# Pacing the loads of a fused attention and mixture-of-experts kernel by memsets on VectorE, with a third buffer for values

## The chip, the cores and the metric

The kernel runs on one core of one Trainium2 chip. Five engines take part: TensorE (PE in the profile; PEld is its weight load), VectorE (DVE), ScalarE (ACT), GpSimd (POOL) and SyncE (SP). SP computes nothing; it issues nearly all DMA transfers, in the order of the program. The metric is the time of one execution on the device in microseconds (us), as a median over runs.

## The reference

Block-sparse attention over 4 batches, 8 heads, 768 positions and 64 channels, followed by a mixture of 8 experts in which each token goes to one expert. Positions form 24 blocks of 32. A query block sees its own block and its two neighbours, the first and the last block, and three drawn blocks; the first and the last query block see everything.

```python
mask = np.abs(blk_i - blk_j) <= 1
mask = mask | (blk_i == 0) | (blk_j == 0) | (blk_i == n_blocks - 1) | (blk_j == n_blocks - 1)
for qb in range(n_blocks):
    for kb in sampled_blocks[qb]:
        mask[qb*32:(qb+1)*32, kb*32:(kb+1)*32] = True
scores = np.where(mask, scale * q @ k.T, -1e9)
x = softmax(scores) @ v                      # heads side by side: 3072 tokens x 512
e_idx = np.argmax(x @ w_gate + modality_bias[modality_id], axis=1)
out[e_idx == e] = gate_w * (np.maximum(x @ w1[e], 0) @ w2[e])
```

## The kernel before

**Attention by tiles.** The batches are worked in two halves of two batches. In each half the two outer query blocks (0 and 23) are the dense part, 8 items of two heads; the other 22 query blocks go two at a time as 11 sparse tiles, so there are 22 sparse tiles, g = 0 to 21. A sparse tile has four items, (n, b): query block n of the pair, batch b of the half. All items stand in one list of 104: first the 8 dense items of half 0, then the 88 sparse ones, with the 8 dense items of half 1 put in two at a time after the sparse items 21, 29, 45 and 47 (DENSE_AFTER).

**Ticks.** The list is run as a software pipeline. In tick t the step `op` is made for the item t - LAG[op]: for a sparse item the scores S (L528) at its own tick, the mask M (L536, VectorE) one later, the exponential X (L544, ACT) two, the transposes T (L553) and their copy A (L558, ACT) four, the weighing W of shared values (L575) five, the weighing V of own values (L584) seven, the division O (L438) eight, a turning Y ten, and the gate G (L601) thirteen later. W, V, O, Y and G are made once per tile, at its last item. Within a tick the order is `OXTSMGVAYW`, with numbered places between; `side(t, f, place)` hangs other work on a place of a tick. The first 14 ticks are written out by hand as a list of tokens (START). The order of each engine's instructions is the order of the program (a manual schedule); semaphores come from the data alone. So SP, which has no part in the arithmetic, issues a load as soon as it has come to it and its buffer is free.

**Loads of a sparse tile**, all on SP. With `last(g)` the tick of a tile's last item:

- Queries, `fetch_q` (L142), 256 KB into one of three `q_raw` buffers, with the drawn block numbers read into registers (`own_numbers`, L508), at last(g-2), place 3. For tiles without dense items between them this is 5 ticks ahead of the tile's first scores.
- Neighbour values, `fetch_v` (L486 to L492), two loads of 128 KB, at last(g-2) + 8. In the first two tiles of a half two more loads bring the blocks 0 and 23, which then stay in the buffer; the other two neighbour blocks are copied from the buffer of the tile before by GpSimd, `share_v` (L499), at last(g-2) + 11.
- Own (drawn) values, `fetch_own` (L516), six loads of 128 KB, at last(g-2) + 9 and + 10.

The value buffers `vbuf` are two, slots 7 and 8, so the loads of tile g wait until tile g-2 has been weighed, which is at last(g-2) + 7. The weighing of the tile's own values is at last(g-2) + 15 where no dense items come between, that of the shared ones two earlier. Keys lie in the chip as a whole (`kd`); `share_k` (L462 to L477, GpSimd) copies those of a tile together.

**Dense loads of half 1**: keys (L154) and values (L160) in pieces of 256 KB, at ticks written in DENSE_IN, 14 to 59.

**Probabilities**: the copies A go to `at`, five buffers, for sparse items (L558) and to `ad`, four buffers cut from slot 4, for dense ones (L414).

**From attention to experts.** When both tiles of a pair have been gated, a generator `routing` is put in a queue (`fillers`) of which a few steps are made in each tick (ten in half 0, seven in half 1). It chooses the expert, computes the gate weight (`write`, L311), lets LATER = 19 steps pass, issues two x writes of 256 KB to `x_d` in DRAM (L323), and then goes on to rank the rows (`chain`, `rank`). When 16 of the 24 row tiles are ranked, `choose(0)` picks the expert with the most rows; with that begins `early_groups`, stepped once per tick. It fetches the first weights (`fetch`, L704 and L708, 512 KB each, two at its first step, the third to fifth at its ticks 6, 9 and 12), splits each into two parts (L712 ACT, L713 VectorE or GpSimd) and gathers the rows of group 0 (`gather`, L718). Its matmuls (L736 to L738, L751 to L753) begin when the last tile has been weighed. Then 10 further groups of 256 rows and a last half group follow, each with 8 weights of 512 KB.

**Slots** are pieces of on-chip memory of 12 KB per partition, used one after another: 0, 1, 2 and 9 for dense keys, 2 and 3 for dense values, 4 for `ad`, 5 and 6 for the sparse keys, 7 and 8 for sparse values; later all of them for weights and rows (`expert_slots`).

## Time and profile before

| | us |
|---|---|
| median of 3 runs (lowest, highest) | 546.74 (543.19, 548.45) |
| the profiled execution | 548.88 |
| its span, first to last instruction | 547.1 |
| mean granted TensorE clock | 0.986 |
| DMA on SP's queue | 105.02 MB, 64.1% of 16 engines' span |

The profiled execution is the source of all rows. Its time is 1.8 us more than its span and 2.1 us more than the median. The page gives busy time per engine and 40 slices of 13.7 us, in which a digit is a tenth. A row of the timeline is start, duration, engine, line, operation, and in brackets the idle time before it with what ended it: `[0.86 <-DMA slot<-v]` is 0.86 us in which TensorE waited for a load of values. "Issue" is idle time for which the profile shows no releaser. SPq is SP's queue of DMA issues. Attention runs until about 240 us, the first two groups of the experts until about 290, the rest to the end.

### The profile page before, as it was taken

The numbers are of one execution on the slowest core, as the hardware profiler recorded it, in microseconds if no ns is written. First come the engines' busy times: TensorE is split into PE (matmuls) and PEld (weight loads), VectorE is DVE, ScalarE is ACT, GpSimd is POOL, SyncE is SP. The second block draws the span as 40 slices with busy tenths as digits, with TensorE's granted clock in tenths as the row PEclk, the third lists the DMA queues.
The fourth block names the chain that finished last, engine by engine and source line by source line (L and its number), as shares of the span: only waits on it lengthen the run. The fifth ranks groups of instructions, "written<-read, shape, count | busy, mean of one in ns | idle before, by whom it ended". The sixth has DMA issues, their size and how long they took to land.

```text
span 547.1 us, 18936 instructions
## 1 busy us (share of the span) xinstructions
PE 517.6 (95%) x7274; PEld 435.0 (80%) x7274; DVE 373.2 (68%) x1129; ACT 337.4 (62%) x768; POOL 222.2 (41%) x453
## 2 busy tenths in 40 slices
PE   7999899999999997889999999999999999999994
PEld 5567666777778775778879898998989899898973
DVE  4895667778679997776984756556566555656652
ACT  2789866978878987644444555545455554654561
POOL 1758754867458884540454031230303203031121
PEclk9899999999999999799999999999999999999998
DMA  8994898869975779936778875766758566675730
GB/s 283 307 237 120 243 229 223 241 190 231 224 207 144 200 205 270 239 97 248 266 250 268 278 248 187 253 218 229 244 173 269 191 228 236 220 242 191 258 121 22
DMA packets 48690, 119.43 MB, mean 218 GB/s; under 512 B 7632, under 2 KB 7760, under 8 KB 48592
## 3 DMA queue, kind: packets, MB, share of 16 engines
q1 hardware_dynamic: 44512, 105.02, 64.1%
q0 software_dynamic: 4080, 13.12, 6.6%
q8 instruction: 59, 0.97, 0.8%
q14 instruction: 39, 0.32, 0.2%
HBM read 105.52 MB, written 12.86 MB: 216 GB/s over the span
## 4 chain that ended last, share of the span: by engine, by line
PE 71%; DVE 10%; DMA 8%; issue 5%; POOL 2%; ACT 1%; SPq 1%; POOLq 1%; DVEq 0%; ACTq 0%
PE bank L753 8%; PE bank L752 7%; PE bank L751 7%; PE bank L736 7%; PE bank L738 7%; PE bank L737 7%; PE bank L553 5%; PE bank L528 5%; DMA slot<-v 4%; PE bank L575 2%; PE bank L584 2%; PE bank L725 2%; DMA slot<-kD 2%; DVE slot L713 2%; PE bank L601 2%
## 5 line engine op out<-in xcount | busy, mean ns | idle before, releaser
L713 DVE TENSOR_TENSOR slot<-slot 128x1024 fp32r<-128x1024 f32 x96 | 120.2, 1257 | 92.5 <-ACT slot L712 92.3
L712 ACT CAST slot<-slot 128x1024 fp32r<-128x1024 f32 x104 | 108.1, 1048 | 103.0 <-PE bank L737 50.7
L738 PE MATMUL bank<-slot 128*128 128x256 f32 x384 | 107.8, 281 | 0.9 <-DVE slot L713 0.9
L736 PE MATMUL bank<-slot 128*128 128x256 f32 x384 | 108.4, 282 | 0.0
L737 PE MATMUL bank<-slot 128*128 128x256 f32 x384 | 107.6, 280 | 0.0
L762 POOL DMA_INDIRECT out<-slot,si x21 | 21.2, 1008 | 184.1 <-ACT slot L758 181.1
L544 ACT ACTIVATE a<-y,mn 128x256 f32<-128x256 f32 x176 | 88.6, 510 | 7.1 <-DVE mn L536 6.9
L753 PE MATMUL bank<-slot 128*128 128x512 f32 x200 | 79.1, 396 | 1.3 <-DVE slot L744 1.3
L751 PE MATMUL bank<-slot 128*128 128x512 f32 x200 | 80.0, 400 | 0.0
L752 PE MATMUL bank<-slot 128*128 128x512 f32 x200 | 79.1, 395 | 0.0
L738 PEld LDWEIGHTS bank<-slot 128*128 128x128 f32 x384 | 72.2, 188 | 1.1 <-DVE slot L713 1.1
L736 PEld LDWEIGHTS bank<-slot 128*128 128x128 f32 x384 | 72.2, 188 | 0.6
L737 PEld LDWEIGHTS bank<-slot 128*128 128x128 f32 x384 | 72.2, 188 | 0.4
L536 DVE CUSTOM_DVE_ANT_1 y<-bank,smask 128x256 f32<-128x256 f32 x176 | 66.1, 417 | 0.5
L477 POOL COPY slot<-slot 128x128 f32 x264 | 63.6, 294 | 6.0 <-issue 6.0
L558 ACT COPY at<-bank 128x512 f32<-128x512 f32 x88 | 50.7, 577 | 11.8 <-PE bank L553 11.7
L499 POOL TENSOR_SCALAR slot<-slot 32x1024 f32<-32x1024 f32 x40 | 41.7, 1042 | 29.9 <-PE bank L584 11.6
L553 PE MATMUL bank<-ident,a 128*128 128x128 f32 x352 | 53.2, 284 | 0.2 <-DVE mn L536 0.2
L528 PE MATMUL bank<-slot,q_raw 64*32 64x256 f32 x1408 | 50.3, 382 | 1.8 <-DMA q_raw<-qH 0.8
L753 PEld LDWEIGHTS bank<-slot 128*128 128x128 f32 x200 | 37.6, 188 | 10.8 <-DVE slot L744 1.7
L752 PEld LDWEIGHTS bank<-slot 128*128 128x128 f32 x200 | 37.6, 188 | 8.1 <-DVE slot L713 0.4
L751 PEld LDWEIGHTS bank<-slot 128*128 128x128 f32 x200 | 37.6, 188 | 7.9 <-ACT slot L911 0.3
(290 smaller groups left out, 849.9 us busy)
## 6 DMA issues: line engine op xcount, KB each, us to landing
slot<-w SPq DMA_DIRECT2D x105, 512.0 KB
slot<-v SPq DMA_DIRECT2D x180, 128.0 KB
x_d<-xr SPq DMA_DIRECT2D x22, 256.5 KB
q_raw<-qH SPq DMA_DIRECT2D x22, 256.0 KB
slot<-v SPq DMA_DIRECT2D x16, 256.0 KB
slot<-kD SPq DMA_DIRECT2D x13, 256.0 KB
slot<-v SPq DMA_DIRECT2D x4, 768.0 KB
slot<-kD SPq DMA_DIRECT2D x3, 768.0 KB
```

The lines of the kernel that those rows point to most:

```text
L528: nc.tensor.matmul(sp[u][32 * pr:32 * pr + 32, b * 256:(b + 1) * 256], lhsT=q[r, b * NPAIR + pr, n, :], rhs=kv[r, s0:s0 + 8, b, pr, :], st ...
L536: nc.vector.tensor_tensor_reduce(y[:, u, :].rearrange("p (s f) -> p s f", s=8), sp[u][:, b * 256:(b + 1) * 256].rearrange("p (s f) -> p s ...
L544: nc.scalar.activation(a[:, u, :], y[:, u, :], AF.Exp, bias=mn[:, u:u + 1], scale=-1.0, accum_out=total[:, u:u + 1])
L553: nc.tensor.transpose(tp[:, k:k + P], a[:, u, c * P:(c + 1) * P], ident)
L712: nc.scalar.copy(h, staged(n))
L713: (eng or (nc.gpsimd if n in POOL_SPLITS else nc.vector)).tensor_tensor(l, staged(n), h.bitcast(F32), ALU.subtract)
L736: nc.tensor.matmul(o, lhsT=h[:, fs], rhs=xh[g % 2][:, c, :], start=c == 0 and f % 2 == 0, stop=False)
L737: nc.tensor.matmul(o, lhsT=h[:, fs], rhs=xl[g % 2][:, c, :], start=False, stop=False)
L738: nc.tensor.matmul(o, lhsT=l[:, fs], rhs=xh[g % 2][:, c, :], start=False, stop=c == 3 and f % 2 == 1)
L751: nc.tensor.matmul(o, lhsT=hh[0][:, f, ts_], rhs=h[:, fs], start=f == 0, stop=False)
L752: nc.tensor.matmul(o, lhsT=hh[0][:, f, ts_], rhs=l[:, fs], start=False, stop=False)
L753: nc.tensor.matmul(o, lhsT=hl[f // 4][:, f % 4, ts_], rhs=h[:, fs], start=False, stop=f == 7)
```

## The change

- **Pacing.** `pace(spot)` is a memset of one element on VectorE. It is put ahead of query loads (from tile 2 on), of the second neighbour load (L492) and of each of the two groups of own loads (from tile 2 on), on an element that the load then overwrites. The load so waits until VectorE has come to that place in its own program.
- **Third buffer.** `vbuf` has three buffers (slots 8, 7, 4). The two neighbour loads go to last(g-2) + 4 and + 7, the own loads to + 5 and + 6. The blocks 0 and 23 are loaded in the first three tiles of a half.
- **Probabilities.** `ad` is gone; dense and sparse items share six `at` buffers.
- **x writes.** The 19 steps go, and ranking follows at once. `put_row` hangs the two writes of a pair on ticks 2 past a multiple of 4 (counted from the first sparse tick), four ticks apart; past tick NI + 8 they are issued at once. `gather` asserts that the rows it needs have been written.
- **First weights.** Until attention ends, `load` makes one fetch per step, and each is half a weight (256 KB).
- **Slots.** The tables of the beginning are in slot 9, the first two weight stages and gathered rows in slot 0 in place of 4, and the split weights in slot 4 in place of 0.

```diff
-VL = (8, 1)
+VL = ((4, 7), (7, 1))
 VS = (11, 7)
-VG = ((9, 6), (10, 3))
+VG = ((5, 1), (6, 1))
...
-NAT, NXR = 5, 5
-LATER = 19
+NAT, NXR = 6, 5
+XD = (2, 6)
...
-        vbuf = [slot(7 + n)[:, 0:3072].rearrange("p (c f) -> p c f", c=3) for n in range(2)]
+        vbuf = [slot(n)[:, 0:3072].rearrange("p (c f) -> p c f", c=3) for n in (8, 7, 4)]
...
+        def pace(spot):
+            nc.vector.memset(spot, 0.0)
+
-        def fetch_q(half, m):
+        def fetch_q(half, m, paced=False):
             q_raw = work.tile([P, 2, HB * NPAIR * 32], F32, name="q_raw", bufs=3)
+            if paced:
+                pace(q_raw[0:1, 0, 0:1])
             nc.sync.dma_start(q_raw.rearrange("p n f -> p (n f)"), qH[half, m])
...
-        blk_raw = const.tile([P, NB * 3 * 2], I32, name="blk_raw")
+        setup = slot(9)
+        blk_raw = setup[:, 0:NB * 6].bitcast(I32)
...
-            for _ in range(LATER):
-                yield
             for n in range(2):
-                nc.sync.dma_start(x_d[(tau + n) * P:(tau + n + 1) * P, :], xrs[n])
+                put_row(n, tau + n, xrs[n])
...
-        def fetch_v(m, half):
+        def fetch_v(m, half, ns=(0, 1)):
             i, g = 2 * m + 1, half * NM + m
-            vg = vbuf[g % 2]
+            vg = vbuf[g % 3]
...
-            if m < 2:
+            if m < 3 and 0 in ns:
...
-            nc.sync.dma_start(vg[0:32, 2, :], vrow[:, i + 2, :])
-            nc.sync.dma_start(vg[96:P, 1, :], vrow[:, i + 1, :])
+            for n in ns:
+                vn = vg[0:32, 2, :] if n == 0 else vg[96:P, 1, :]
+                if n and g > 1:
+                    pace(vn[0:1, 0:1])
+                nc.sync.dma_start(vn, vrow[:, i + 2 - n, :])
...
+            if g > 1:
+                pace(vg[32 * n:32 * n + 1, 2 * n, 0:1])
+            for k in ks:
+                reg = own[g][3 * n + k]
                 nc.sync.dma_start(vg[32 * (k + n):32 * (k + n) + 32, 2 * n, :], vrow[:, bass.ds(reg, 1), :].rearrange("p j f -> p (j f)"))
...
-            def load(nf, ns):
+            def load(nf, ns, slow=False):
...
-                        fetch(f)
-                        now["fetch"] += 1
+                        if slow or now["half"]:
+                            fetch(f, now["half"])
+                            now["half"] ^= 1
+                        else:
+                            fetch(f)
+                        now["fetch"] += not now["half"]
+                        if slow:
+                            return
...
-                load(p + 2, p)
+                load(p + 2, p, True)
...
+        def put_row(n, tau, xr):
+            def put():
+                nc.sync.dma_start(x_d[tau * P:(tau + 1) * P, :], xr)
+                written.add(tau)
+            t_ = t + 1
+            while (t_ - at["s", 0, 0, 0, 0]) % 4 != XD[0]:
+                t_ += 1
+            t_ += 4 * n
+            if t_ < NI + 8:
+                side(t_, put, XD[1])
+            else:
+                put()
+
         def q_load(m, half):
-            qraw[m, half] = fetch_q(half, m)
+            qraw[m, half] = fetch_q(half, m, (m, half) > (1, 0) or half > 0)
```

## The prediction

> **What bounds the kernel now.** I read the page first (busy time, slices), then the table of windows by stage, then the timelines of TensorE and of SP's queue where TensorE is idle, and last the groups of VectorE.

> ```profile
> span 547.1 us, 18936 instructions
> ...
> PE 517.6 (95%) x7274; PEld 435.0 (80%) x7274; DVE 373.2 (68%) x1129; ACT 337.4 (62%) x768; POOL 222.2 (41%) x453
> ...
> PE   7999899999999997889999999999999999999994
> ...
> PEclk9899999999999999799999999999999999999998
> DMA  8994898869975779936778875766758566675730
> ```

> TensorE is busy for 95% of the span, so at most some 30 us are there to win, and the slices say where: at the very start, in slices 5 to 7, and in slices 15 to 17, where the granted clock falls too. Where the DMA digits are 9 the PE digits drop.

> ```profile
> 60.00:110.00 50.00, 45.93 (x1108) 33.63 (x1098) 35.76 (x156) 38.03 (x123) 31.44 (x85) 1.00 0.90 238
> 163.90:193.60 29.70, 29.70 (x839) 23.34 (x837) 27.14 (x127) 26.24 (x86) 25.05 (x68) 1.00 0.60 165
> 193.60:224.40 30.80, 24.68 (x691) 19.02 (x692) 27.23 (x135) 23.95 (x75) 19.73 (x39) 1.00 0.94 248
> 224.70:231.60 6.90, 6.90 (x75) 6.40 (x67) 4.27 (x13) 3.38 (x9) 4.44 (x3) 0.51 0.93 239
> 231.60:239.70 8.10, 7.32 (x236) 6.33 (x234) 6.24 (x45) 5.49 (x13) 0.88 (x1) 1.00 0.59 152
> 239.70:292.60 52.90, 50.58 (x375) 44.74 (x374) 39.67 (x103) 22.72 (x31) 19.57 (x12) 1.00 0.66 229
> 292.60:530.00 237.40, 237.40 (x1537) 214.91 (x1537) 144.30 (x154) 125.03 (x154) 50.98 (x43) 1.00 0.68 227
> ```

> Columns: stretch, its length, busy us (and count) of PE, PEld, DVE, ACT, POOL, granted clock, DMA share, GB/s. From 292.6 on TensorE never stops: the experts are bound by it, and whatever is won before passes through to the end one for one. Stage 163.9 to 193.6 is also full. The losses: 50.00 - 45.93 = 4.07 us in 60 to 110; 30.80 - 24.68 = 6.12 us in 193.6 to 224.4; 6.90 us at a clock of 0.51, which is 0.49 x 6.90 = 3.4 us; 8.10 - 7.32 = 0.78 us after that; 52.90 - 50.58 = 2.3 us in 239.7 to 292.6. What the second and fourth consist of:

> ```profile
> 163.84 1.08 PE L584 MATMUL bank<-slot,at 128*32 128x64 f32 x64
> 193.60:224.40 30.80, 24.68 (x691) 19.02 (x692) 27.23 (x135) 23.95 (x75) 19.73 (x39) 1.00 0.94 248
> ...
> 201.14 0.25 PE L568 MATMUL bank<-rexp,fold 128*32 128x8 f32 x8 [0.39 <-ACT at L558]
> 202.40 1.09 PE L584 MATMUL bank<-slot,at 128*32 128x64 f32 x62 [0.86 <-DMA slot<-v]
> 211.10 0.36 PE L584 MATMUL bank<-slot,at 128*32 128x64 f32 x2 [0.63 <-DMA slot<-v]
> 212.85 1.09 PE L584 MATMUL bank<-slot,at 128*32 128x64 f32 x62 [1.39 <-DMA slot<-v]
> 215.73 1.10 PE L528 MATMUL bank<-slot,q_raw 64*32 64x256 f32 x32 [0.76 <-DMA q_raw<-qH]
> 218.03 0.92 PE L575 MATMUL bank<-slot,at 128*64 128x64 f32 x24 [0.35 <-issue]
> 224.40 0.42 PE L584 MATMUL bank<-slot,at 128*32 128x64 f32 x14 [1.64 <-issue]
> 238.63 1.09 PE L584 MATMUL bank<-slot,at 128*32 128x64 f32 x62 [0.79 <-issue]
> ```

> The first two rows are the weighing of own values (L584) of tiles 12 and 16: four tiles in 29.76 us, so 7.44 us for a tile and 1.86 us for a tick (four to a tile). After them the weighing of tiles 17 and 18 waits for value loads (0.86 + 0.63 + 1.39 = 2.88 us), the scores of tile 21 wait 0.76 us for queries, and 0.39 + 0.35 + 1.64 + 0.79 = 3.17 us are ACT and "issue". Why the loads are late stands in SP's queue:

> ```profile
> 181.65 0.38 SPq L491 DMA_DIRECT2D slot<-v  x1
> 189.96 0.35 SPq L491 DMA_DIRECT2D slot<-v  x1
> 198.82 0.38 SPq L491 DMA_DIRECT2D slot<-v  x1
> 202.34 0.91 SPq L704 DMA_DIRECT2D slot<-w  x2
> 203.44 3.38 SPq L516 DMA_DIRECT2D slot<-v  x6
> 209.88 0.35 SPq L142 DMA_DIRECT2D q_raw<-qH  x1
> ...
> SPq L491 <- PE bank L584: 15.4, 5, 5.6
> ```

> L491 is the first value load of a tile. With two buffers it may go only when the tile two before has been weighed: five waits, 15.4 us. From tile 16 on SP is simply slower than TensorE: L491 at 181.65 and 198.82 is 17.17 us for two tiles, 8.59 us each with one pair of x writes, against 7.44. So it falls behind 1.15 us per tile until, at 202.34, two weights of 512 KB go in ahead of tile 19's six own loads.

> **The change, part by part.** *Third buffer, earlier loads.* Own loads move from ticks 9 and 10 to 5 and 6 after the last item of the tile two before, and the weighing stands at tick 15: their lead grows from 5 or 6 ticks (9.3 us) to 9 or 10 (17 us). The neighbour loads gain 4 ticks and 1. At 203.44 the own loads took 3.38 us to issue, and the slowest row for a landing is the queries' (issued at 209.88, waited for until 215.73: 5.85 us). 17 us hold both and over 7 us of lateness besides, so I take the 2.88 us as gone (ends: 0 and 2.88).

> *SP's queue.* The change removes nothing from it: eight value loads, one query load with its register load, and one x write per tile are still issued, and four more value loads (rows 0 and 23 for a third buffer) and five more halves of weights come in. Each paced load now waits for VectorE, and all later entries stand behind it: own loads, x writes, weights and dense keys. The loads with the shortest lead are the queries, 5 ticks or 9.3 us, unchanged. From tile 15 to the query load of tile 21 SP can lose 5 x 1.15 = 5.8 us and 4 halves x 0.91/2 = 1.8 us (row at 202.34), 7.6 us; with 5.85 us of landing that is 4.1 us more than the lead. The wait for tile 21's queries, 0.76 us now, is then between 0 and 4.1 us; SP loses part of this lateness wherever the dense items lengthen a tile, so I take the middle, 2.0 us: cost 1.3 us net.

> *Memsets.* 20 for queries, 19 for neighbour values, 40 for own values: 79 on VectorE, four to a tile.

> ```profile
> L214 DVE MEMSET smask<- 128x1 f32 x1 | 0.1, 59 | 0.1
> L444 DVE RECIPROCAL rd<-rd 128x1 f32<-128x1 f32 x16 | 2.6, 164 | 0.6
> ...
> 150.88 1.07 PE L584 MATMUL bank<-slot,at 128*32 128x64 f32 x60
> 152.77 0.31 PE L584 MATMUL bank<-slot,at 128*32 128x64 f32 x4 [0.82 <-issue]
> ```

> A memset of one column took 59 ns: 79 x 59 = 4.7 us, and 4 x 59 = 0.24 us per tile. VectorE idles (29.70 - 27.14)/4 = 0.64 us per tile in the full stage, so it is hidden; at the price of the next small operation (164 ns) it would be 0.66 us and just not. Should VectorE wait in a memset, the masked scores (L536) behind it stop, then ACT, then TensorE. What it must wait for is old: the weighing three tiles back lies two ticks earlier in program order, and GpSimd's sharing of that buffer four ticks. I take 0.3 us; ends 0 and 4.7, all of it.

> *Dense and sparse probabilities share six buffers in place of five and four.* Counting allocations, only one is tight: tile 12's first copy (L558) must now wait for tile 11's weighing of the same tick. The last two rows are that weighing; until now the copy could run beside it. Between 0 and the 2.2 us from 150.88 to 153.08; ACT has two ticks until its next result is due, so 0.3 us.

> *x writes.* Issued two ticks after the gates or more, one by one, in place of 19 steps later, as a pair. Same bytes, same queue, 0; the rows are gathered later still. Because those steps no longer stand ahead of the ranking, the choice of the first expert and its weights come about 19/7 = 2.7 ticks (5 us) earlier, and that lies in the same crowded stretch; its price is in SP's 7.6 us. *Weights in halves:* one half a tick in place of 512 KB at once; the bytes between two value loads halve. *Small tables in slot 9, first stages in slot 0, weights in slot 4:* the slots are free long before; 0.

> *Issue and ACT waits* (3.17 us): no part of the change names them, but they stand where the DMA share is 0.94. Between 0 and 3.17; half, 1.6 us.

> *The dense stretch.* Of the 4.07 us in 60 to 110 the rows give one load wait:

> ```profile
> 92.23 0.66 PE L375 MATMUL bank<-slot,qd 64*64 64x256 f32 x8 [0.43 <-DMA slot<-kD]
> ```

> 0.4 us for dense keys, taken as gone. The rest waits for banks and engines. Ends: 2 us gained, or 2 us lost if the start, where SP now waits for the memsets of tiles 2 and 3 in place of running ahead, hands on its lateness.

> *Clock.* 3.4 us at 0.51. It fell at 224.7, after 6.1 us of gaps in 31 us, and was 1.00 in all full stages; I take it as back. [...]

> **The sum.** 2.9 + 1.6 + 3.4 + 0.4 - 1.3 - 0.3 - 0.3 = 6.4 us gained. The profiled execution took 548.9 us, 2.1 us over the median of the runs shown (546.74), so it gives 542.5 for itself; carried to the median, 540.3, and I say 540.5.

> **The rivals.** *Clock stays low* (0.15): all else as above, 540.3 + 3.4 = 543.7. For it: the last two tiles leave TensorE little to do with or without waits. *The waits only move* (0.13): DMA runs at 248 GB/s and a share of 0.94 in 193.6 to 224.4, and the weights now begin 5 us sooner in just that stretch. If the value waits and the clock stay, the sum is 0.1: 546.6. Against it: DMA's share is 0.60 in the 30 us before, room for loads that come earlier. *SP's queue becomes the bound* (0.13), the other side: paced by VectorE it can't use a quiet moment, and at 8.59 us a tile the query loads turn late after (9.3 - 5.85)/1.15 = 3 tiles. It decides once the query waits pass the 4.9 us won elsewhere without the clock. With tiles 14 to 21 and the halves that is 8 x 1.15 + 1.8 - 3.45 = 7.6 us, and 2 us in the dense stretch, 4 with the memsets in full: 11.6 to 13.6, less 4.9: 6.7 to 8.7 us slower, 554. Against it: own loads no longer hold SP up, 15.4 us of waits. *Everything clears* (0.15): SP's lateness is absorbed, all of 2.88 + 0.76 + 3.17 + 3.4, and 2 us of the dense stretch: 12.2 us, 534.5. The forecast keeps 0.44.

> **How the numbers follow.** About 1% (5.5 us) is what a measurement of this kernel can tell from no change: under 541.3 is faster, over 552.2 slower. Faster: 0.6 of the forecast's 0.44, the 0.15 of the full clearing and a little of the clock's: 0.43. Slower: most of SP's 0.13: 0.11. Within 1%: 0.46. The forecast's own range, by its ends, is 536 to 545. From 533.5 to 549 it takes in the clearing, the clock and the moved waits, and leaves out SP's case and tails.

> **What would show it.** L584 without a DMA wait after 193.6, tiles 7.4 us apart up to the last: the buffer is right. A wait of L528 on q_raw of 1 to 3 us at tile 20 or 21: SP's term is right; such waits from tile 15 on, or before 110 us, make SP the bound and me wrong. VectorE's memsets at some 60 ns with no idle time before them on PE or POOL: the pacing is free. The clock at 1.00 up to the first expert matmul, which comes at 239.7 now and should come near 234: the clock's term. If the first expert matmul comes earlier by what I say but the end does not, the stage up to 292.6 has taken it back.

## The result, and the profile after

The changed kernel took 570.33 us (median of 4 runs, 568.22 to 576.74), the kernel before 545.50 us on the same chip (median of 4, 543.19 to 548.45). The ratio is 1.0425, with a 95% interval of 1.0364 to 1.0486: some 23 us slower. The prediction said 540.5, and not over 549. The profiled execution took 571.51 us. Ratios leave out executions counted as slow (here the one of 576.74), which the medians include; the profiles of e3 and e14 below are of such executions.

In code and profile the lines have moved: masked scores L536 are now L543, scores L528 are L535, the weighing of own values L584 is L591, sharing of values L499 is L503 and of keys L477 is L476, queries L142 are L145, own loads L516 are L523, the gather L718 is L731, the split L712 and L713 are L724 and L725, the x write L323 is L1192. The memsets are L139. Experiments shift them by up to five more.

The page of the changed kernel, to be set against the page shown ahead:

```profile
span 569.6 us, 19125 instructions
...
PE 521.2 (92%) x7274; PEld 436.5 (77%) x7274; DVE 377.3 (66%) x1209; ACT 338.1 (59%) x768; POOL 223.8 (39%) x452
...
PE   7798798989999998588889999999999999999994
...
PEclk9999798999999999689999999999999999999998
```

TensorE's busy time grew by only 3.6 us, from 517.6 to 521.2, while the span grew by 22.5. So TensorE stands idle for longer, and where it is busy part of that is at half clock (0.50): the PEclk row has dents in slices 5, 7, 17 and 18, where before there were two, in slices 2 and 17. To find where the time goes, take the start of each tile's weighing of own values (the first row of its block at L584 or L591 in TensorE's timeline):

| tile | before, us | after, us | later by |
|---|---|---|---|
| 1 | 51.8 | 53.3 | 1.5 |
| 2 | 59.6 | 68.1 | 8.5 |
| 7 | 113.8 | 122.3 | 8.5 |
| 8 | 121.1 | 132.9 | 11.8 |
| 12 | 163.8 | 175.6 | 11.8 |
| 18 | 211.1 | 226.5 | 15.4 |
| 19 | 221.5 | 248.8 | 27.3 |
| first expert matmul | 239.7 | 260.3 | 20.6 |
| last matmul | 539.1 | 561.6 | 22.5 |

Three steps stand out: tile 2 (7 us), tile 8 (3.3 us, and 3.6 more between 12 and 18), and tile 19 (11.9 us, of which 6.7 come back before the first expert matmul). The table of windows for these stretches, first the changed kernel, then the kernel before (length, busy PE, PEld, DVE, ACT, POOL, clock, DMA share, GB/s):

```profile
44.90:68.10 23.20, 17.37 (x417) 13.54 (x416) 9.96 (x59) 14.29 (x47) 14.57 (x38) 0.85 0.87 215
122.30:132.90 10.60, 8.71 (x210) 6.84 (x210) 8.37 (x46) 5.95 (x20) 8.43 (x21) 0.84 0.72 209
226.50:248.80 22.30, 13.17 (x229) 9.65 (x233) 16.21 (x48) 10.73 (x32) 17.40 (x25) 0.73 0.71 198
313.00:550.00 237.00, 237.00 (x1539) 214.33 (x1539) 144.90 (x154) 125.80 (x156) 49.47 (x42) 1.00 0.69 229
```

```profile
44.20:59.60 15.40, 14.93 (x419) 11.71 (x423) 9.83 (x50) 14.00 (x47) 13.16 (x37) 1.00 0.56 164
113.80:121.10 7.30, 7.30 (x214) 5.67 (x218) 6.44 (x31) 6.03 (x21) 5.83 (x18) 1.00 0.44 139
211.10:221.50 10.40, 7.90 (x204) 5.96 (x205) 8.44 (x38) 6.65 (x21) 4.08 (x3) 1.00 1.03 259
```

From 313 on TensorE is full, as before: the experts pass the lateness on, one for one (on the critical chain the first block of eight at L725, now L738, after 300 us starts at 310.00 before and 332.94 after, 22.94 us later, the last at 520.29 and 542.81, 22.52 us later). What TensorE waits for in the three places, from its timeline (start, length, the idle time before it in brackets):

```profile
60.47 1.11 PE L535 MATMUL bank<-slot,q_raw 64*32 64x256 f32 x16 [5.08 <-DMA q_raw<-qH]
...
125.92 0.17 PE L331 MATMUL bank<-oh,upper 128*128 128x8 bf16 x1 [1.89 <-DVE oh L306]
...
235.19 0.68 PE L535 MATMUL bank<-slot,q_raw 64*32 64x256 f32 x8 [6.30 <-POOL slot L476]
...
245.67 0.18 PE L331 MATMUL bank<-oh,upper 128*128 128x8 bf16 x1 [2.08 <-ACT a L551]
```

and from its table of waits (us in all, times, longest):

```profile
PE bank L331 <- DVE oh L306: 5.2, 5, 1.9
```

Queries (L535 on q_raw), ranks (L331, which multiply the choice `oh` that VectorE makes), GpSimd's keys (L476), ranks again. The prediction had priced a wait for queries at tile 21 only, and none of the other three. Of the waits for value loads that it priced, L591 has none left.

*The start.* SP's queue in the changed kernel:

```profile
25.73 2.36 SPq L523 DMA_DIRECT2D slot<-v  x5
35.31 0.36 SPq L145 DMA_DIRECT2D q_raw<-qH  x1
...
45.12 0.37 SPq L145 DMA_DIRECT2D q_raw<-qH  x1
46.85 0.79 SPq L485 DMA_DIRECT2D slot<-v  x2
...
48.79 2.22 SPq L523 DMA_DIRECT2D slot<-v  x3
...
51.72 1.33 SPq L523 DMA_DIRECT2D slot<-v  x3
...
54.08 0.37 SPq L145 DMA_DIRECT2D q_raw<-qH  x1
```

and VectorE's timeline just before its second load:

```profile
35.20 0.06 DVE L139 MEMSET q_raw<- 1x1 f32 x1
```

This is the memset of tile 2's queries, reached only at 35.20, behind the dense items and the small tables with which VectorE is full until then (busy 6.81 of the 7.22 us from 28.09 to 35.31). SP stands still from 28.09 to 35.31; before, the same load went out at 27.97, since its buffer had never been used. The queries of tile 4 go out at 54.08 (before: 46.24), TensorE waits for them until 60.47.

*The gather.* GpSimd's timeline, of the changed kernel (its first row is SP's, the x write of row tile 15, the sixteenth of its line) and of the kernel before:

```profile
221.00 0.42 SPq L1192 DMA_DIRECT2D x_d<-xr  x1
...
227.31 1.16 POOL L731 DMA_INDIRECT slot<-x_d,gi_e  x1 [12.84 <-DVE rt L435]
228.78 0.96 POOL L731 DMA_INDIRECT slot<-x_d,gi_e  x1 [0.30 <-DMA slot<-v]
229.75 2.37 POOL L725 TENSOR_TENSOR slot<-slot 128x1024 fp32r<-128x1024 f32 x1
...
233.66 2.90 POOL L476 COPY slot<-slot 128x128 f32 x12
236.65 2.16 POOL L503 TENSOR_SCALAR slot<-slot 32x1024 f32<-32x1024 f32 x2
```

```profile
205.39 2.15 POOL L499 TENSOR_SCALAR slot<-slot 32x1024 f32<-32x1024 f32 x2
207.73 1.18 POOL L718 DMA_INDIRECT slot<-x_d,gi_e  x1 [0.18 <-POOL slot L499]
```

Before, GpSimd shared tile 19's values (L499) at 205.39, some 10 us ahead of their first use (L575 at 218.03, in the timeline shown ahead), and gathered afterwards. Now the gather and the split of the second weight stand ahead of it and of the keys of tile 21 (L476). The gather waits 12.84 us (the trace names VectorE; by the events on its semaphore the x write landed at 226.22, 1.1 us before the gather), and all GpSimd's lead is gone: the keys are ready at 236.56, the values at 238.81. The kernel's own schedule shows why, by the ticks at which the program issues these steps:

| step | before | after |
|---|---|---|
| rank of row tiles 14 and 15 (TensorE) | 88 | 86 |
| x write of row tile 15 (SP) | 88 | 94 |
| rank of row tiles 16 and 17 | 96 | 94 |
| first gather (GpSimd), needs row tiles 0 to 15 | 100 | 97 |
| split of the second weight (GpSimd) | 100 | 97 |
| values of tile 19 shared (GpSimd) | 98 | 98 |

Between the last row written and the first gather lay 12 ticks; now 3, and SP issues that write only at 221.00. In the trace GpSimd stands 12.84 us in front of keys and values (L476, L503), which then ran without a wait of their own.

### The profile page after: what moved, and what is told of

Its sections match the earlier page's. It is cut to its first block, busy times and chain, and to the rows that moved or that the text cites. A ratio compares the mean times of both kernels' runs of the same rounds, so it can differ in the third digit from the quotient of the medians.

```text
span 569.6 us, 19125 instructions
## 1 busy us (share of the span) xinstructions
PE 521.2 (92%) x7274; PEld 436.5 (77%) x7274; DVE 377.3 (66%) x1209; ACT 338.1 (59%) x768; POOL 223.8 (39%) x452
## 4 chain that ended last, share of the span: by engine, by line
PE 69%; DVE 13%; DMA 8%; issue 4%; ACT 3%; POOL 1%; SPq 1%; DVEq 0%; POOLq 0%; ACTq 0%
PE bank L751 8%; PE bank L749 8%; PE bank L750 8%; PE bank L764 7%; PE bank L765 7%; PE bank L766 7%; PE bank L535 5%; DMA slot<-v 5%; PE bank L560 4%; PE bank L582 3%; PE bank L591 2%; PE bank L738 2%; DVE y L543 2%; ACT a L551 2%; PE bank L608 1%
## 5 line engine op out<-in xcount | busy, mean ns | idle before, releaser
L725 DVE TENSOR_TENSOR slot<-slot 128x1024 fp32r<-128x1024 f32 x96 | 122.3, 1279 | 94.2 <-ACT slot L724 94.0
L724 ACT CAST slot<-slot 128x1024 fp32r<-128x1024 f32 x104 | 108.1, 1048 | 102.5 <-PE bank L750 50.4
L751 PEld LDWEIGHTS bank<-slot 128*128 128x128 f32 x384 | 72.3, 188 | 2.0 <-DVE slot L725 2.0
L749 PEld LDWEIGHTS bank<-slot 128*128 128x128 f32 x384 | 72.3, 188 | 0.5
L750 PEld LDWEIGHTS bank<-slot 128*128 128x128 f32 x384 | 72.3, 188 | 0.5
L543 DVE CUSTOM_DVE_ANT_1 y<-bank,smask 128x256 f32<-128x256 f32 x176 | 66.9, 419 | 1.1
L476 POOL COPY slot<-slot 128x128 f32 x264 | 63.9, 298 | 5.9 <-issue 5.9
L535 PE MATMUL bank<-slot,q_raw 64*32 64x256 f32 x1408 | 52.5, 405 | 12.7 <-POOL slot L476 6.3
L503 POOL TENSOR_SCALAR slot<-slot 32x1024 f32<-32x1024 f32 x40 | 41.8, 1045 | 15.2 <-DVE mn L543 6.4
L766 PEld LDWEIGHTS bank<-slot 128*128 128x128 f32 x200 | 37.5, 188 | 9.4 <-DVE slot L931 0.4
L765 PEld LDWEIGHTS bank<-slot 128*128 128x128 f32 x200 | 37.6, 188 | 8.6 <-DVE slot L725 1.0
L535 PEld LDWEIGHTS bank<-slot,q_raw 64*32 64x32 f32 x1408 | 23.2, 110 | 26.7 <-issue 8.8
## 6 DMA issues: line engine op xcount, KB each, us to landing
slot<-v SPq DMA_DIRECT2D x4, 768.0 KB, 14.3
```

What stands on the lines that cost most here:

```text
L535: nc.tensor.matmul(sp[u][32 * pr:32 * pr + 32, b * 256:(b + 1) * 256], lhsT=q[r, b * NPAIR + pr, n, :], rhs=kv[r, s0:s0 + 8, b, pr, :], st ...
L543: nc.vector.tensor_tensor_reduce(y[:, u, :].rearrange("p (s f) -> p s f", s=8), sp[u][:, b * 256:(b + 1) * 256].rearrange("p (s f) -> p s ...
L724: nc.scalar.copy(h, staged(n))
L725: (eng or (nc.gpsimd if n in POOL_SPLITS else nc.vector)).tensor_tensor(l, staged(n), h.bitcast(F32), ALU.subtract)
L749: nc.tensor.matmul(o, lhsT=h[:, fs], rhs=xh[g % 2][:, c, :], start=c == 0 and f % 2 == 0, stop=False)
L750: nc.tensor.matmul(o, lhsT=h[:, fs], rhs=xl[g % 2][:, c, :], start=False, stop=False)
```

## The experiments

The theory after the result (A in the expectations): three separate losses, the start, the ranks and the order on GpSimd, the last two both from the 19 steps taken out. The rival (B): SP's queue is the bound throughout, so that a loss taken away returns elsewhere. Each run is set against the kernel before on its own chip.

| run | ratio to before (95% interval) | median, us |
|---|---|---|
| the changed kernel | 1.0425 (1.0364 to 1.0486) | 570.33 |
| e1: query loads unpaced | 1.0359 (1.0287 to 1.0430) | 564.50 |
| e2: 19 steps back, behind the x writes | 1.0143 (1.0070 to 1.0215) | 552.48 |
| e3: gather three ticks later | 1.0319 (1.0236 to 1.0401) | 562.94 |
| e4: x writes at once | 1.0447 (1.0365 to 1.0529) | 569.09 |
| e6: e1 and e2 together | 1.0012 (0.9976 to 1.0048) | 546.38 |
| e7: gather and splits three ticks later | 1.0294 (1.0243 to 1.0344) | 561.02 |
| e8: no memsets, steps and x writes as before | 1.0023 (0.9980 to 1.0065) | 545.34 |
| e13: e2, and two query loads unpaced | 1.0007 (0.9966 to 1.0048) | 546.78 |
| e17: e8, and dense queries loaded sooner | 1.0050 (1.0014 to 1.0087) | 546.85 |
| from the kernel before: | | |
| e9: memsets ahead of the queries | 1.0008 (0.9978 to 1.0037) | 545.00 |
| e10: 19 steps out | 1.0279 (1.0206 to 1.0351) | 561.79 |
| e12: e10, gather and splits at their old ticks | 1.0165 (1.0100 to 1.0230) | 555.84 |
| e14: ranks, choice of experts and first weights sooner, all else at its tick | 1.0150 (1.0096 to 1.0204) | 554.18 |
| e15: e14, gather and splits sooner too | 1.0262 (1.0223 to 1.0302) | 559.15 |
| e16: x writes two ticks sooner | 1.0163 (1.0129 to 1.0197) | 553.47 |
| e11: nothing changed, one execution | | 550.13 |

**The start: e1, e9, e13.**

```diff
 def q_load(m, half):
-    qraw[m, half] = fetch_q(half, m, (m, half) > (1, 0) or half > 0)
+    qraw[m, half] = fetch_q(half, m)
```

> The changed kernel without its 20 memsets ahead of the query loads; all else as changed. Theory A, three separate losses in the changed kernel (the start, where SP stands 7 us in the memset of tile 2's queries; the ranks, where TensorE waits for VectorE; the gather, which holds GpSimd 12.8 us): the first goes, the weighing of own values of tile 2 comes back from 68.1 to about 60 us, the half-speed stretch at 59 to 66 us goes with it, and the whole takes 560 to 563 us. Theory B, SP's queue is the bound from start to end, so that a delay taken away in one place comes back in the next: tile 2 is earlier, tile 16 is not, and the whole stays within 2 us of 570.

Tile 2 is weighed at 59.4 us again, tile 16 at 200.6 (after: 207.7) and tile 18 at 218.5 (226.5): 8.0 us earlier, so B falls. But tile 18 to 19 takes 23.3 us, and TensorE waits 8.2 us at the ranks where it waited 5.2 on VectorE: part of what was won is lost at the next two waits, and 564.5 is above A's 560 to 563. The intervals of e1 and of the changed kernel overlap, so the size of this gain is uncertain. A likely reason is that a start that comes sooner meets a gather that still needs a late x write.

In e9 the memset was put into the kernel before:

```diff
 q_raw = work.tile(...)
+if (m, half) > (1, 0) or half > 0:
+    nc.vector.memset(q_raw[0:1, 0, 0:1], 0.0)
 nc.sync.dma_start(q_raw.rearrange("p n f -> p (n f)"), qH[half, m])
```

> The kernel before with one thing added: the 20 one-element memsets ahead of the query loads. Theory A: the start stall is theirs alone; SP stands some 7 us ahead of tile 2's queries, tile 2 is weighed at 66 to 68 in place of 59.6, the half clock at 59 to 66 appears, and the whole takes 549 to 553 us. Rival (the stall needs the earlier value loads too, or is made good in the dense ticks at 85 to 93): within 2 us of before.

No loss at all, so the part of A that gave the stall to the memsets alone is wrong. SP's queue in e9:

```profile
34.52 0.36 SPq L144 DMA_DIRECT2D q_raw<-qH  x1
...
43.57 0.37 SPq L144 DMA_DIRECT2D q_raw<-qH  x1
45.31 0.80 SPq L156 DMA_DIRECT2D slot<-kD  x2
...
47.57 0.35 SPq L144 DMA_DIRECT2D q_raw<-qH  x1
```

SP stands until 34.52, nearly as long as in the changed kernel. But tile 4's queries follow tile 3's after 4.00 us, against 8.96: the changed kernel has between them six own loads (L523, 3.55 us) and two first and last blocks (0.79 us) that the third buffer lets go earlier. Either is harmless alone (e9: query memsets without the buffer, 1.0008; e6 below: the buffer, with the memsets of the value loads and without those of the queries, 1.0012); together they make the query load late. That the value loads in between are the reason is read from the two queues; no run moved them alone. e13 keeps 18 of the 20 memsets and drops those of tiles 2 and 3:

```diff
-    qraw[m, half] = fetch_q(half, m, (m, half) > (1, 0) or half > 0)
+    qraw[m, half] = fetch_q(half, m, m > 3 or half > 0)
     # and the 19 steps back, as in e2
```

> The changed kernel with the 19 steps back (as in that run, 1.0143) and the query loads of tiles 2 and 3 without a memset; the 18 later ones keep theirs. Theory A: all that the query memsets cost is the start: with the first two gone the time is that of the run with none, ratio 1.000 to 1.004, 544 to 547 us. Rival: the 18 others cost too, by holding SP (seven waits of 15 us in the changed kernel): 1.008 to 1.014.

1.0007 against 1.0143 with all twenty: the two first memsets are the whole price, some 1.4% or 7.4 us, and the 18 others cost nothing that can be measured.

**The steps: e2, e3, e4, e7.**

```diff
 for n in range(2):
     put_row(n, tau + n, xrs[n])
+for _ in range(19):
+    yield
```

> The changed kernel with the 19 empty steps put back, between the x writes and the ranking; the x writes stay at the ticks of the changed kernel. Ranks come one to two ticks later, the first gather at tick 100 in place of 97, behind the sharing of tile 19's values on GpSimd. Theory A (three separate losses): TensorE's waits of 5 to 7 us at the ranks (L331) go, and so do most of the 6.3 us that the scores of tile 21 wait for GpSimd, with the half clock behind both: 548 to 555 us; the start stays late (tile 2 weighed at 68). Theory B (SP's queue is the bound): the ranks' waits are replaced by waits for loads, 567 to 571.

As A said: 2.8% less than the changed kernel, about 15 us, the largest single part. Of TensorE's waits at the ranks 0.2 us is left. The start stays late, but by another tile than A said: tile 2 is weighed at 62.9, tile 3 at 76.3 as in the changed kernel. e3 and e7 ask what part of it is GpSimd's queue:

```diff
-TICKS = (6, 9, 12)
+TICKS = (9, 12, 15)       # e7 only
...
-    rows(0)
+    if tick >= 12:
+        rows(0)
```

> The changed kernel with the first gather alone put from tick 97 to tick 100, behind the sharing of tile 19's values; ranks, x writes and memsets as changed. Theory A: the wait of 12.8 us in front of the gather no longer holds up that sharing nor the keys of tile 21, the distance from the weighing of tile 18 to that of tile 19 falls from 22 to about 11 us, the half clock at 233 to 244 goes, and the whole takes 557 to 562 us; the ranks' waits stay. Theory B (SP's queue): 568 to 571.

> The changed kernel with the first gather at tick 100 and the splits of the first three weights three ticks later (100, 103, 106), so that on GpSimd neither stands ahead of the sharing of tile 19's values; ranks, choice, x writes and memsets stay as changed. With the gather alone moved, GpSimd still waited 11.5 us in the split ahead of that sharing. Theory A: tile 18 to tile 19 falls to 10 to 12 us (from 22.3; 14.3 with the gather alone), half clock at 233 to 244 gone, waits of TensorE at the ranks (L331) still 5 to 8 us: 556 to 560 us. If the ranks' own place is what the steps took away: no better than with the gather alone, 563.

Tile 18 to 19 takes 14.3 us in both, and the whole 1.0319 and 1.0294. e3 is at the edge of what A said; e7 reached neither its 10 to 12 us nor its 556 to 560. What is left in that stretch of e7 is mainly one wait of 4.0 us at the ranks; over the whole run L331 waits 10.7 us, more than A's 5 to 8. In e4 the rows are written in time:

```diff
 for n in range(2):
-    put_row(n, tau + n, xrs[n])
+    nc.sync.dma_start(x_d[(tau + n) * P:(tau + n + 1) * P, :], xrs[n])
+    written.add(tau + n)
```

> The changed kernel with the x writes issued as a pair at the step where they fall due, in place of one by one four ticks apart; the row of token tile 15 goes out at tick 86 in place of 94, the gather stays at tick 97. Theory A: the gather finds its rows written and holds GpSimd no longer: 557 to 562 us as with the gather put later, with the ranks' waits unchanged. If instead the gather's place on GpSimd is what hurts and not the rows, or SP's queue is the bound: 568 to 571.

GpSimd's timeline in e4 and, behind it, in e3:

```profile
215.92 1.17 POOL L732 DMA_INDIRECT slot<-x_d,gi_e  x1 [0.31 <-DMA slot<-v]
...
227.09 2.38 POOL L726 TENSOR_TENSOR slot<-slot 128x1024 fp32r<-128x1024 f32 x1 [8.73 <-ACT slot L725]
```

```profile
224.67 2.39 POOL L725 TENSOR_TENSOR slot<-slot 128x1024 fp32r<-128x1024 f32 x1 [11.52 <-ACT slot L724]
```

The gather now waits 0.31 us, and the whole is no faster. Behind it in the same queue stands the split of the second weight, which waits 8.73 us for what ACT makes of that weight in its own order (L725 in e4, L724 in e3); in e3, where the gather is out of the way, the split waits 11.52 us. Tile 18 to 19 takes 17.8 us in e4, against 22.3 in the changed kernel, so the late rows have a part in that stretch, but the loss does not hang on them. GpSimd ran some 10 us ahead of TensorE; each of these two steps needs what another engine makes late, and either one, put ahead of the sharing, ends that lead.

**The same from the other side: e10, e12, e14, e15, e16.** e10 takes the 19 steps out of the kernel before, and nothing else:

```diff
-for _ in range(LATER):
-    yield
 for n in range(2):
     nc.sync.dma_start(x_d[(tau + n) * P:(tau + n + 1) * P, :], xrs[n])
```

> The kernel before with one thing taken out: the 19 empty steps ahead of the x writes (these still go at once, in pairs). Theory A: these steps are the larger part of the loss, by themselves: ranks come while VectorE is still choosing, TensorE waits 5 to 10 us at L331, and on GpSimd the first gather and the split of the second weight come ahead of the sharing of tile 19's values: 555 to 561 us, a ratio of 1.02 to 1.03. Rival: without the late start and the late x writes of the changed kernel the order does no harm: within 3 us of before.

1.0279: the steps are worth as much in the kernel before as e2 found in the changed one (1.0425 less 1.0143 is 0.0282). e12 is e10 with the gather and the splits at their old ticks, as in e7:

> The kernel before without the 19 steps, but with the first gather held at its tick (100) and the splits of the first weights three ticks later, where they stood: the ranks, the choice and the first fetches come sooner, the order on GpSimd stays. Theory A: of the loss of the run without the steps the waits at the ranks remain, 5 to 9 us: 550 to 555, ratio 1.01 to 1.017. If the order on GpSimd is all: within 2 us of before; if the ranks are all: as the run without the steps.

The number is A's, and so are the waits at the ranks (7.5 us); the trace shows one wait more. In e10 and e12 the x writes also move, from tick 27 to 25, and there SP has the dense queries of the second half (`qd`) behind them. In the timelines of SP and of TensorE in e12:

```profile
64.82 0.39 SPq L321 DMA_DIRECT2D x_d<-xr  x1
65.26 0.46 SPq L147 DMA_DIRECT2D qd<-qD  x1
...
71.18 2.84 PE L373 MATMUL bank<-slot,qd 64*64 64x512 f32 x16 [5.70 <-issue]
```

TensorE idles 5.70 us, put down to "issue", and goes on at 71.18 with the matmul of `qd`, 5.92 us after that load was issued at 65.26; that it waited for the load is inferred from this. In the changed kernel the first x write is at tick 26, behind that load. e14 and e15 keep the x writes at their ticks:

```diff
-for _ in range(LATER):
-    yield
-for n in range(2):
-    nc.sync.dma_start(x_d[(tau + n) * P:(tau + n + 1) * P, :], xrs[n])
+def put():
+    for n in range(2):
+        nc.sync.dma_start(x_d[(tau + n) * P:(tau + n + 1) * P, :], xrs[n])
+side(t + 2, put, 6) if t + 2 < NI else put()
 # e14 only: TICKS and gather as in e7
```

> The kernel before with the ranks (and the choice of experts and the first fetches behind them) without the 19 steps, while the x writes go out at the ticks where they stood, the first gather and the first splits too. Theory A (three parts: ranks 4 to 7 us, order on GpSimd 6 us, x writes ahead of the dense queries 3 to 5 us): waits at L329-or-near of 4 to 8 us in all, no wait at the dense queries at 71, ratio 1.007 to 1.013. Rival B (the ranks are all of the 1.0165): 1.014 to 1.019. Rival C (the x writes are all of it): within 0.004 of 1.

> As the run with the ranks alone, and the first gather (tick 97) and the first splits (94, 97, 100) ahead of the sharing of tile 19's values on GpSimd, as without the steps; x writes at their old ticks. Theory A: 6 us more than the ranks alone, 1.018 to 1.024; tile 18 to 19 takes 16 to 19 us in place of 10 to 13. Rival: the order on GpSimd costs only where rows are written late; then as the ranks alone.

e14 is at 1.0150, 8 us: inside what rival B gave, but its interval reaches into A's 1.007 to 1.013, so the two are not told apart; rival C falls.

e14 moved the choice of experts and the first two weight loads along with the ranks (tick 88 for 91). That the ranks cost by themselves shows earlier in the traces: from tile 7 to tile 8, at some 120 us and long before these loads, every profiled execution with the ranks sooner takes 9.3 to 10.6 us, every one with the ranks at their old ticks 7.1 to 8.3, and up to 300 us TensorE waits 4.0 to 10.7 us for `oh` in the former and 0.2 us in the latter. What the earlier loads add was not tried alone.

In e15 the order on GpSimd adds 1.1% (6 us), a little more than A gave it, and tile 18 to 19 takes 17.2 us where e14 took 11.6, both as A said. The x writes at their old ticks made no difference that can be measured (e14 against e12: 1.0150 and 1.0165; e15 against e10: 1.0262 and 1.0279), so the wait of 5.70 us did not reach the end there. Both waits in TensorE's timeline of e15 (ranks are L334 here, scores L531):

```profile
118.38 0.17 PE L334 MATMUL bank<-oh,upper 128*128 128x8 bf16 x1 [1.92 <-DVE oh L304]
...
222.00 0.88 PE L531 MATMUL bank<-slot,q_raw 64*32 64x256 f32 x23 [2.17 <-POOL slot L480]
```

and the ranks in its table of waits:

```profile
PE bank L334 <- DVE oh L304: 5.4, 6, 1.9
```

e16 moves the x writes alone, by putting the 19 steps behind them:

> The kernel before with the 19 steps put behind the x writes in place of ahead of them: pairs of x writes go out two ticks sooner, ranks, choice, fetches and gather stay. Theory A: the first pair stands ahead of the dense queries on SP, TensorE waits 3 to 6 us at 68 to 71 us (tile 2 to 3 takes 13 to 15 us in place of 9 to 10), ratio 1.005 to 1.010. Rival: the wait at the dense queries comes and goes without it; within 0.004 of 1.

1.0163, more than A's 1.005 to 1.010. Its profiled execution shows the wait at `qd` (3.20 us at 68.68, put down to ACT there) but was the shortest of five, 548.5 against a median of 553.5, so where the rest goes was not seen and stays open. Tile 2 to 3 took 10.9 us in it, not A's 13 to 15. x writes two ticks sooner cost 1.6% by themselves and nothing on top of the ranks: the parts do not add up, 1.5, 1.1 and 1.6% being more than the 2.8% of e10, and the reason is not known.

**What is left of the change: e6, e8, e11, e17.**

> Both together: no memsets ahead of the query loads, and the 19 empty steps back between the x writes and the ranking. Theory A (losses apart: start, ranks, order on GpSimd): the unpaced queries brought tile 18 forward by 8.0 us (226.5 to 218.5), of which a longer wait behind the gather took back 1 to 2; without that wait all 8 should reach the end, from 552 to 544 to 546 us. Theory B (SP's queue is the bound): no more than with the steps alone, 550 to 553.

With e1 and e2 together the loss is gone: 1.0012, near A's 544 to 546 us and not B's 550 to 553. Taken singly, e1 gave 0.0066 and e2 0.0282, which would leave 1.008; with the steps back the unpaced queries are worth 0.0131 (1.0143 less 1.0012), twice as much, as A had it: no gather takes part of it back (though the 0.0066 is itself not clear of the noise). e8 goes further, to the buffer alone: `pace` does nothing, the steps stand ahead of paired x writes.

```diff
-    nc.vector.memset(spot, 0.0)
+    pass
...
-    put_row(n, tau + n, xrs[n])
+    # after the 19 steps, as in the kernel before
+    nc.sync.dma_start(x_d[(tau + n) * P:(tau + n + 1) * P, :], xrs[n])
```

> The changed kernel with no memsets at all, with the 19 steps back ahead of the x writes and these in pairs, as before the change: what is left of the change is the third value buffer with its earlier loads, the six shared buffers, the halves and the slots. Theory A (the buffer is right and its gain was hidden by the three losses): 537 to 541 us, the first expert matmul at 234 to 237. Rival: the gain is not there because the earlier loads crowd SP's queue, queries late by 1 to 4 us at tiles 17 to 21: 543 to 548.

> The kernel before, unchanged, profiled once more. Theory A: the waits of tiles 17 and 18 for value loads (2.9 us) and the half clock behind tile 18 (6.8 us at half speed) are of the one execution that the prediction read; in another the first expert matmul comes 2 to 5 us sooner than 239.7 and some of both is missing, and so the third buffer has little to gain. Rival: both are there again, within 1 us.

e8 is at 545.34 us, in its rival's range. The rival's reason is not in the trace: no scores wait for queries, and the first expert matmul comes at 235.7, where A had put it. e11 is between its two: 1.7 us of waits for values in place of 2.9 and 3.4 us of half clock behind tile 18 in place of 6.8, so some of both is missing; but its first expert matmul comes at 241.9, later than 239.7. The stretch from the weighing of tile 14 to that of tile 21, in the tables of windows of e8 and of e11, which is the kernel before:

```profile
178.10:234.40 56.30, 50.59 (x1355) 39.79 (x1353) 50.81 (x241) 43.42 (x134) 38.26 (x77) 1.00 0.78 207
```

```profile
182.90:239.10 56.20, 51.35 (x1353) 41.16 (x1353) 51.08 (x244) 44.06 (x135) 37.73 (x77) 0.97 0.85 235
```

TensorE's waits inside that stretch, of e8 (the weighing is L594) and of e11 (L584):

```profile
PE bank L594 <- issue: 2.1, 3, 1.1
PE bank L585 <- ACT at L568: 1.2, 1, 1.2
```

```profile
PE bank L584 <- DMA slot<-v: 1.7, 3, 1.3
```

TensorE takes 56.3 us with the third buffer and 56.2 without. In e11 1.7 us of it are waits of the weighing for value loads, and the clock is at 0.97. In e8 there is neither; TensorE idles 2.1 us at "issue" in the same weighing and 1.2 us for one of ACT's copies. In this pair the loads came earlier, and other waits were as long. But single executions scatter by more than the gain looked for: the same stretch took 58.6 us in the execution of the kernel before shown ahead, and 55.1 in e9, which has no third buffer either. What decides is the ratio of e8: by its interval the buffer, with the rest of the change that e8 keeps, wins at most 0.2%, about 1 us. Why it wins no more is argued from one pair and not shown. Last, e17:

```diff
-Q_IN = 25
+Q_IN = 18     # on top of e8
```

> The kernel with the third buffer only (no memsets, steps and paired x writes as before the change), and the dense queries of the second half loaded at tick 18 in place of 25. Theory A: the dense stretch from tile 2 to tile 5 is bound by what SP brings last, the dense queries among it; loaded earlier it wins 1 to 4 us there, 0.992 to 0.998. Rival: DMA itself is full there (share 0.93), what is put ahead makes the next load late: 0.998 to 1.006.

1.0050: nothing won, perhaps a little lost. No run came out measurably under the kernel before.

## Why the prediction was wrong

*The step that failed* is the paragraph on x writes: "Same bytes, same queue, 0; the rows are gathered later still." and, for the 19 steps, "its price is in SP's 7.6 us". The rows are not gathered later but three ticks sooner (97 for 100), while they are written six ticks later (94 for 88). And taking out the steps had a price that SP's queue does not show: they had held TensorE's ranks back until VectorE's choice was made, and GpSimd's gather and split behind its sharing. e15 measures ranks and order at 1.0262, e2 gives 15 us back. The zero for the x writes themselves stands in the changed kernel (e4: 1.0447 against 1.0425); in the kernel before it is open (e16). The working went through SP's queue only, and not through those of TensorE and GpSimd; the ticks of gather and sharing could have been counted from the code, and the 10 us by which GpSimd was ahead stood in GpSimd's timeline of the kernel before.

*The start* was named, "2 us lost if the start, where SP now waits for the memsets of tiles 2 and 3 in place of running ahead, hands on its lateness", as an end, and not taken. It was the right place, and it cost some 7.4 us (e13 against e2). The working looked at what the memset waits for in its buffer ("old"), and not at what VectorE has ahead of it in its own queue, full until 35.20.

*SP's queue becomes the bound* (0.13, 554) had the right side and, in part, the wrong engine. The sign named for it came: a wait of L535 for queries before 110 us, 5.08 us at 60.47. But SP's rate was not the bound: with 18 query memsets, 59 value memsets and the single x writes all still there, e13 is at 1.0007. Its sum does not follow from its terms either: read plainly, 7.6 us and 2 to 4 us are 9.6 to 11.6, not 11.6 to 13.6, which would make it 552.

*Third buffer, 2.88 us gone*: the waits went, as said (L591 waits for no value load). The gain did not come: e8 wins at most 0.2%, and in its trace other microseconds stand at ACT and "issue". That is the rival "the waits only move" in its result, though not by its condition, that the value waits stay. The 1.6 us to be won from issue and ACT waits did not come either: in that stretch e8 has 4.8 us of them, e11 2.6 and the execution shown ahead 2.3.

*Clock, 3.4 us back*: wrong in the changed kernel, where half clock covers 27.3 us of the first 300, in place of 10.2 (6.8 of them behind tile 18). In e8 the profiled execution had none there, and its runs were no shorter than those of the kernel before. e11 had 3.4 us of it behind tile 18 and 10.2 in the dense stretch. So the 3.4 us were read from one execution and counted as if each had them.

*Memsets, 0.3*: right, apart from the start. Their group rows:

```profile
L139 DVE MEMSET slot<- 1x1 f32 x59 | 3.5, 59 | 2.2
L139 DVE MEMSET q_raw<- 1x1 f32 x20 | 1.2, 59 | 0.1
```

79 of them, 59 ns each, 4.7 us on VectorE. e6 (with the 59 for values) and e8 (with none) are at 1.0012 and 1.0023, inside each other's intervals. *Halves, slots, shared buffers*: in e8 all three are there at 1.0023 (at most 1.0065), beside a buffer whose waits are gone; a cost of more than some 0.6% would need a gain of the buffer to hide it, and none was seen. One reading was too strong: "Where the DMA digits are 9 the PE digits drop" holds for two of the seven nines on that page, slices 16 and 17.

## What to carry to other kernels

A gap in the program that looks empty can be what keeps an in-order queue running ahead, as the 19 steps kept GpSimd some 10 us ahead here. Before taking it out, list for each engine what moves past what, and how far ahead of its consumer that engine runs now; a step that needs another engine's present result belongs behind the work that the lead is for (ahead of the sharing the gather waited 12.84 us in the changed kernel, the split 8.73 us in e4). The memset that paced tile 2's queries made SP's queue wait for what VectorE had ahead of it, 7.22 us from 28.09 to 35.31, so pace only loads with slack, and none where VectorE is still full, as it was here at the start (busy 6.81 of those 7.22 us).

## What the runs showed of the hardware

```profile
89.96:93.37 3.41, 1.55 (x31) 1.31 (x31) 1.84 (x11) 2.76 (x10) 2.54 (x11) 1.00 0.93 246
93.37:96.78 3.41, 3.12 (x55) 1.92 (x56) 1.25 (x7) 1.68 (x5) 2.08 (x2) 0.50 0.99 269
...
223.08:226.49 3.41, 2.21 (x48) 1.44 (x48) 3.15 (x21) 3.41 (x10) 0.00 (x0) 1.00 0.73 224
226.49:229.90 3.41, 2.40 (x80) 1.97 (x80) 2.55 (x13) 3.41 (x12) 2.27 (x3) 1.00 1.01 246
```

1.86 us idle of 3.41, and the next window is at 0.50; 1.20 us idle, and it stays at 1.00. So a wait of about 2 us could cost up to 1.7 us more where half speed followed it (an estimate from these traces: one window of 3.41 us at 0.50; eight transposes of the kernel before, L553, took 1.97 us at 224.76 with the clock at 0.50 and 1.09 us at 172.46 with it at 1.00). That may be why e14 lost 8 us where A gave the ranks 4 to 7; it was not shown.
